# Splitting a two-engine weight conversion into two steps emitted apart, and moving all squares to one engine

## The chip, the cores and the metric

The kernel runs on one core of a Trainium2 chip. Of its engines three matter here: TensorE does the matrix products, ScalarE and VectorE work on whole arrays (tiles). They and the DMA queues, which load and store, run side by side. PSUM is the memory that the products are written to, SBUF the on-chip memory that holds the tiles. "Half clock" is short for a granted TensorE clock near 0.50 in a trace; "issue" of a load is the moment it is sent. The metric is the device time of one execution in microseconds (us). Executions of one kernel usually agree within 1 us, some differ by 3. All ratios are to runs of the kernel before on the same chip, in the same rounds, and each is good to about 0.0015 either way.

## The reference, cut to what matters

```python
# attention without softmax: q, k, v are (8, 8, 576, 64)
kv  = einsum('bhsd,bhse->bhde', k, v)
o   = einsum('bhsd,bhde->bhse', q, kv)
x   = (o / sqrt(mean(o * o, -1) + 1e-6) * g_norm)   # then (4608, 512)
# star-ReLU block: w_in (512, 2048), w_out (2048, 512), given as float64
h   = x @ w_in
g   = s * maximum(h, 0) ** 2 + b
out = g @ w_out
```

The weights arrive as 64-bit floats and have to be turned into 32-bit ones on the chip, once, in 16 tiles of 1 MB. That conversion is what the change is about.

## The kernel before

Both products use a Strassen-like scheme with seven products in place of eight. TensorE works through nine "units" of 512 tokens; in the first, the weights are converted while they are first used. A unit's first product has four blocks s of 512 hidden columns with seven products each (x1, z2, x6, y7, x5, x3, y4). In the traces, each of these is a group of 8 matmul records (4 calls, two records a call) and takes 1.73 us undisturbed.

The conversion of a tile: ScalarE works in place on the high and the low words of the raw tile, VectorE then shifts and adds them into the weight tile:

```python
def round_w(i, dst):
    raw = w_raw.pop(i)
    ...
    nc.scalar.activation(hi, hi, AF.Prelu, scale=2.0**-112, alpha=-(2.0**32))
    nc.scalar.activation(lo, lo, AF.Copy, scale=2.0**-29)
    db = dst.bitcast(U32)
    nc.vector.tensor_scalar(out=db, in0=pairs[:, :, 1], scalar1=3, scalar2=None, op0=ALU.logical_shift_left)
    nc.vector.tensor_tensor(out=db, in0=db, in1=lo, op=ALU.add)
```

Three raw buffers (`tag="raw", bufs=3`) take the loads; the next load is sent after each conversion. Tiles 0 to 7 are w_in (two for each block), 8 to 15 w_out. The products of a block and what they leave to the other engines:

```python
rp = ctx.enter_context(tc.tile_pool(name="rp", bufs=1))      # one buffer for each tag
...
def keep(name, src, tag):                                    # PSUM -> SBUF, ScalarE
    st[name] = rp.tile([P, 2, TB], FP32, name=name, tag=tag)
    nc.scalar.copy(st[name], src)
def x1(): ... mm1_product(1, u, s, st["x"], True);  keep("r1", st["x"], "ra")
def z2(): ... add(t, ps, st["r1"]);                 relu_sq(t, u == 0)
def x6(): ... mm1_product(6, u, s, st["x"], False); keep("r2", st["x"], "rb")
def x5(): ... mm1_product(5, u, s, st["x"], False); keep("r4", st["x"], "ra")
          ... add(t, st["y"], st["r4"]);            relu_sq(t, False)
def x3(): ... # relu on ScalarE, product t*t on VectorE
def y4(): ... add(t, st["y"], st["r2"]);            relu_sq(t, u == 0)
```

x6, x5 and x3 add to the PSUM bank that the copy before them reads, so TensorE can't go on until `r1`, `r2`, `r4` have been copied. `relu_sq(t, True)` is a relu and a square on ScalarE, `relu_sq(t, False)` one fused operation on VectorE. In the traces each of these engines works in the order of emission.

## Time and profile before

| | before |
|---|---|
| median, lowest to highest of 3 runs | 1031.41 us, 1031.16 to 1031.42 |
| span of the profiled execution | 1029.7 us |
| first unit's first product, start to end (35.04 to 113.52 us) | 78.5 us |
| its work at 1.73 us for each of 28 groups | 48.4 us |
| TensorE busy, ScalarE busy, VectorE busy (whole span) | 985.9, 214.4, 444.9 us |

The first row is the time to improve. The third against the fourth is what can be had: about 30 us, all in one early stretch. After it TensorE is busy almost without a break (910.9 of 915.3 us). The bias product (the star-ReLU's b times the output weights) starts where the stretch ends, so its start is the mark by which I compare the traces. The lines of the profile itself are in the prediction.

### The profile page before, as it was taken

What the parts mean: (1) busy time and instruction counts of PE and PEld (TensorE: products, weight loads), DVE (VectorE), ACT (ScalarE), POOL (GpSimd) and SP (SyncE); (2) the same over time, 40 slices, a digit from 0 to 9 for tenths busy, and PEclk for the clock granted to TensorE, in tenths of its full rate; (3) what the DMA queues carried; (4) which work ended last, traced back from release to release, by engine and by line L of the source; (5) the groups of instructions that cost most, each with busy time, mean ns of one, the idle gap of its engine ahead of it and who ended that gap; (6) DMA issues with size and microseconds to landing.
All of it is one profiled execution on the core that took longest, in us unless ns stands there. A gap on an engine that the chain in (4) does not pass through costs nothing.

```text
span 1029.7 us, 13548 instructions
## 1 busy us (share of the span) xinstructions
PE 985.9 (96%) x5824; PEld 860.0 (84%) x5824; DVE 444.9 (43%) x725; ACT 214.4 (21%) x370; POOL 1.6 (0%) x8
## 2 busy tenths in 40 slices
PE   4668899999999999999999999999999999999998
PEld 4557488888888888888888888888888888888887
DVE  0665663445234533453345334433344334524441
ACT  2545512121212121212121212111211121111100
POOL 0000000000000000000000000000000000000000
PEclk9889999999999999999999999999999999999999
DMA  9344781772255125513452325232503250324032
GB/s 249 129 164 141 203 280 52 207 172 82 82 164 134 58 107 153 136 50 123 129 128 65 140 79 147 73 126 76 167 1 123 68 178 1 123 62 143 1 123 82
DMA packets 75244, 121.47 MB, mean 118 GB/s; under 512 B 41904, under 2 KB 49072, under 8 KB 68016
## 3 DMA queue, kind: packets, MB, share of 16 engines
q1 hardware_dynamic: 72048, 118.90, 38.6%
q10 hardware_dynamic: 3136, 1.71, 0.8%
q8 instruction: 46, 0.75, 0.3%
q14 instruction: 14, 0.11, 0.0%
HBM read 103.81 MB, written 16.78 MB: 117 GB/s over the span
## 4 chain that ended last, share of the span: by engine, by line
PE 91%; ACT 3%; DVE 2%; DMA 2%; issue 0%; DVEq 0%
PE x_ps L84 51%; PE y_ps L84 26%; PE z_ps L84 8%; PE qT_ps L295 2%; PE kv_ps L272 2%; PE xT_ps L334 1%; PE b_ps L84 1%; ACT w_raw L163 1%; ACT w_raw L162 1%; DMA kv_sb<-in_v_dram 1%; DMA q_sb<-in_q_dram 1%; DVE wb L168 0%; DMA w_raw<-in_moe_w_in_dram 0%; ACT a L378 0%; ACT a L377 0%
## 5 line engine op out<-in xcount | busy, mean ns | idle before, releaser
L84 PE MATMUL x_ps<-w_sb,a 128*128 128x256 f32 x768 | 172.3, 379 | 0.0
L84 PE MATMUL x_ps<-xs,ws 128*128 128x256 f32 x576 | 142.6, 392 | 18.7 <-ACT r L396 14.8
L84 PEld LDWEIGHTS x_ps<-w_sb,a 128*128 128x128 f32 x768 | 144.3, 190 | 18.9 <-issue 0.2
L84 PE MATMUL y_ps<-w_sb,a 128*128 128x256 f32 x640 | 143.4, 379 | 0.0
L84 PEld LDWEIGHTS x_ps<-xs,ws 128*128 128x128 f32 x576 | 112.6, 196 | 36.6 <-ACT r L396 16.5
L84 PE MATMUL y_ps<-xs,wb 128*128 128x256 f32 x576 | 136.8, 380 | 0.0
L396 ACT COPY r<-x_ps 128x512 f32<-128x512 f32 x108 | 63.2, 585 | 331.4 <-PE x_ps L84 329.5
L84 PEld LDWEIGHTS y_ps<-w_sb,a 128*128 128x128 f32 x640 | 119.4, 190 | 15.2 <-issue 0.2
L84 PEld LDWEIGHTS y_ps<-xs,wb 128*128 128x128 f32 x576 | 110.1, 191 | 15.2
L171 DVE TENSOR_TENSOR a<-y_ps,r 128x512 f32<-128x512 f32 x72 | 49.4, 687 | 132.8 <-ACT r L396 132.8
L84 PE MATMUL x_ps<-xT,wa 128*128 128x256 f32 x288 | 70.6, 390 | 2.1 <-DVE wa L168 2.1
L380 DVE SCALAR_TENSOR_TENSOR a<-a 128x512 f32<-128x512 f32 x100 | 69.2, 692 | 3.4
L84 PE MATMUL x_ps<-xT,ws 128*128 128x256 f32 x288 | 68.8, 382 | 0.7 <-ACT r L396 0.7
L84 PE MATMUL z_ps<-xT,wa 128*128 128x256 f32 x288 | 68.0, 379 | 0.0
L84 PEld LDWEIGHTS x_ps<-xT,wa 128*128 128x128 f32 x288 | 56.7, 197 | 10.7 <-DVE wa L168 2.4
L468 DVE SCALAR_TENSOR_TENSOR or<-x_ps,s_col,b_row 128x256 f32<-128x256 f32 x54 | 26.0, 482 | 89.1 <-PE x_ps L84 89.1
L84 PEld LDWEIGHTS x_ps<-xT,ws 128*128 128x128 f32 x288 | 54.1, 190 | 8.9 <-ACT r L396 1.4
L321 DVE TENSOR_REDUCE ss<-xn 128x8 f32<-128x512 f32 x36 | 24.6, 684 | 85.4 <-ACT xn L319 85.3
L84 PEld LDWEIGHTS z_ps<-xT,wa 128*128 128x128 f32 x288 | 54.7, 190 | 7.4
L429 DVE TENSOR_TENSOR a<-a 128x512 f32<-128x512 f32 x36 | 24.9, 692 | 79.3 <-ACT a L428 79.3
L84 PE MATMUL x_ps<-w_sb,s 128*128 128x256 f32 x256 | 57.8, 380 | 0.0
L84 PEld LDWEIGHTS x_ps<-w_sb,s 128*128 128x128 f32 x256 | 47.6, 190 | 6.1 <-issue 0.2
(80 smaller groups left out, 785.4 us busy)
## 6 DMA issues: line engine op xcount, KB each, us to landing
w_sb<-w SPq DMA_DIRECT2D x56, 1024.0 KB, 4.9
kv_sb<-in_k_dram SPq DMA_DIRECT2D x32, 288.0 KB, 5.2
out_dram<-o SPq DMA_DIRECT2D x72, 128.0 KB, 2.3
q_sb<-in_q_dram SPq DMA_DIRECT2D x68, 128.0 KB, 6.0
w_raw<-in_moe_w_in_dram SPq DMA_DIRECT2D x8, 1024.0 KB, 5.6
w_raw<-in_moe_w_out_dram SPq DMA_DIRECT2D x8, 1024.0 KB, 5.0
kv_sb<-in_v_dram SPq DMA_DIRECT2D x28, 288.0 KB, 6.4
w<-w_up SPq DMA_DIRECT2D x4, 1024.0 KB, 7.8
```

The costliest lines, as they stand in the source:

```text
L84: nc.tensor.matmul(o, lhsT=lhsT, rhs=rhs, start=start, stop=stop, skip_group_check=True)
L162: nc.scalar.activation(hi, hi, AF.Prelu, scale=2.0**-112, alpha=-(2.0**32))
L163: nc.scalar.activation(lo, lo, AF.Copy, scale=2.0**-29)
L171: nc.vector.tensor_tensor(out=o, in0=a, in1=b, op=ALU.add)
L272: nc.tensor.matmul(ps[r][l * HB : l * HB + HB, i, :], lhsT=kv[rows, 0, l, j, :], rhs=kv[rows, 1, l, j, :], start=(j == 0), stop=(j == R - 1),)
L295: nc.tensor.transpose(ps[:, p, :], q_in[c][:, 2 * p : 2 * p + 2, :], ident)
L321: nc.vector.reduce_sum(ss, st["xn"], axis=mybir.AxisListType.X)
L334: nc.tensor.transpose(ps[:, p, :], st["xn"][:, 2 * p : 2 * p + 2, :], ident)
L380: nc.vector.scalar_tensor_tensor(t, t, 0.0, t, ALU.max, ALU.mult)
L396: nc.scalar.copy(st[name], src)
L429: nc.vector.tensor_mul(t, t, t)
L468: nc.vector.scalar_tensor_tensor(o, ps, s_col, other, ALU.mult, ALU.add)
```

## The change

Its intent: ScalarE's half of the conversion ("split") is emitted one tile ahead of VectorE's half ("join"), so that VectorE never waits for it, and the squares leave ScalarE, so that it never waits for VectorE. The core of the diff:

```diff
-    def round_w(i, dst):
+    def split_w(i):
         raw = w_raw.pop(i)
...
         nc.scalar.activation(hi, hi, AF.Prelu, scale=2.0**-112, alpha=-(2.0**32))
         nc.scalar.activation(lo, lo, AF.Copy, scale=2.0**-29)
+        w_bits[i] = pairs
+
+    def join_w(i, dst):
+        bits = w_bits.pop(i)
...
-            out=db, in0=pairs[:, :, 1], scalar1=3, scalar2=None, op0=ALU.logical_shift_left
+            out=db, in0=bits[:, :, 1], scalar1=3, scalar2=None, op0=ALU.logical_shift_left
         )
-        nc.vector.tensor_tensor(out=db, in0=db, in1=lo, op=ALU.add)
+        nc.vector.tensor_tensor(out=db, in0=db, in1=bits[:, :, 0], op=ALU.add)
...
-    def relu_sq(t, on_act):
-        if on_act:
-            nc.scalar.activation(t, t, AF.Relu)
-            nc.scalar.activation(t, t, AF.Square)
-        else:
-            nc.vector.scalar_tensor_tensor(t, t, 0.0, t, ALU.max, ALU.mult)
+    def relu_sq(t):
+        nc.vector.scalar_tensor_tensor(t, t, 0.0, t, ALU.max, ALU.mult)
...
     turn[3]()
+    split(0)
     turn_x[0]()
     product[2]()
     turn_x[1]()
+    join(0)
     product[3]()
+    split(1)
     turn_x[2]()
-    convert(0)
-    turn_x[3]()
     first = {s: mm1(0, s) for s in range(NS)}
     first[0]["x1"]()
+    turn_x[3]()
     x_sums(0)
-    convert(1)
+    join(1)
...
-    at_slot = {0: 2, 2: 3, 4: 4, 7: 5, 9: 6, 12: 7, 15: 8, 18: 9, 20: 10, 22: 11, 24: 12, 26: 13, 27: 14}
+    at_slot = {
+        0: [(split, 2)], 1: [(join, 2), (split, 3)], 3: [(join, 3), (split, 4)], 5: [(join, 4)],
+        6: [(split, 5)], 8: [(join, 5), (split, 6)], 10: [(join, 6)], 11: [(split, 7)],
+        12: [(join, 7)], 13: [(split, 8)], 15: [(join, 8), (split, 9)],
...
+        25: [(join, 13), (split, 14)], 27: [(join, 14), (split, 15)],
+    }
```

A load is still sent after each join, and the raw buffers are still three. The diff also moves some joins to other places between the products (join 5 to slot 8 from 7, join 10 to 19 from 20) and the last turn of x behind the first product.

More of the change, by code (lines that the diff above doesn't have):

```diff
@@ L144, in load_w @@
         w_raw[i] = dst
-    def round_w(i, dst):
+    w_bits = {}
+    def split_w(i):
         raw = w_raw.pop(i)
         if not wide:
-            nc.vector.tensor_copy(out=dst, in_=raw)
+            w_bits[i] = raw
             return
@@ L163, in round_w @@
         nc.scalar.activation(lo, lo, AF.Copy, scale=2.0**-29)
+        w_bits[i] = pairs
+    def join_w(i, dst):
+        bits = w_bits.pop(i)
+        if not wide:
+            nc.vector.tensor_copy(out=dst, in_=bits)
+            return
         db = dst.bitcast(U32)
         nc.vector.tensor_scalar(
-            out=db, in0=pairs[:, :, 1], scalar1=3, scalar2=None, op0=ALU.logical_shift_left
+            out=db, in0=bits[:, :, 1], scalar1=3, scalar2=None, op0=ALU.logical_shift_left
         )
-        nc.vector.tensor_tensor(out=db, in0=db, in1=lo, op=ALU.add)
+        nc.vector.tensor_tensor(out=db, in0=db, in1=bits[:, :, 0], op=ALU.add)
     def add(o, a, b):
@@ L177, with join_w_in @@
     wa, wb, ws = {}, {}, {}
-    def round_w_in(s, lower):
+    def join_w_in(s, lower):
         store, base = (wb, FC // 2) if lower else (wa, 0)
         store[s] = wp.tile([P, KC, 2, P], FP32, name=f"w{'ab'[lower]}_{s}")
-        round_w(base + 2 * s, store[s].rearrange("p c b n -> p (c b n)"))
+        join_w(base + 2 * s, store[s].rearrange("p c b n -> p (c b n)"))
     def sum_w_in(s):
@@ L214, with join_w_out @@
     }
-    def round_w_out(s, lower):
+    def join_w_out(s, lower):
         dst = (w_dn if lower else w_up)[:, 2 * s : 2 * s + 2]
-        round_w(FC + (FC // 2 if lower else 0) + 2 * s, dst.rearrange("p b n -> p (b n)"))
+        join_w(FC + (FC // 2 if lower else 0) + 2 * s, dst.rearrange("p b n -> p (b n)"))
     def sum_w_out(i, fn, a, b):
@@ L407, in z2 @@
             add(t, ps, st["r1"])
-            relu_sq(t, u == 0)
+            relu_sq(t)
         def x6():
@@ L422, in x5 @@
             add(t, st["y"], st["r4"])
-            relu_sq(t, False)
+            relu_sq(t)
         def x3():
@@ L437, in y4 @@
             add(t, st["y"], st["r2"])
-            relu_sq(t, u == 0)
+            relu_sq(t)
         return dict(x1=x1, z2=z2, x6=x6, y7=y7, x5=x5, x3=x3, y4=y4)
@@ L593, in send_w, with split, join @@
             sent[0] += 1
-    def convert(n):
-        s, lower = divmod(n % FC, 2)
+    def split(n):
+        split_w(blocks[n])
+    def join(n):
+        s, lower = divmod(n, 2)
         if n < FC // 2:
-            round_w_in(s, lower)
+            join_w_in(s, lower)
             send_w()
@@ L603, in convert @@
         else:
-            round_w_out(s - NS, lower)
+            join_w_out(s - NS, lower)
             send_w()
@@ L664, in loads @@
             load_q(4 * u + 6)
-    at_slot = {0: 2, 2: 3, 4: 4, 7: 5, 9: 6, 12: 7, 15: 8, 18: 9, 20: 10, 22: 11, 24: 12, 26: 13, 27: 14}
+    at_slot = {
+        0: [(split, 2)], 1: [(join, 2), (split, 3)], 3: [(join, 3), (split, 4)], 5: [(join, 4)],
+        6: [(split, 5)], 8: [(join, 5), (split, 6)], 10: [(join, 6)], 11: [(split, 7)],
+        12: [(join, 7)], 13: [(split, 8)], 15: [(join, 8), (split, 9)],
+        17: [(join, 9), (split, 10)], 19: [(join, 10), (split, 11)],
+        21: [(join, 11), (split, 12)], 23: [(join, 12), (split, 13)],
+        25: [(join, 13), (split, 14)], 27: [(join, 14), (split, 15)],
+    }
     for u in range(U):
@@ L689 @@
             if u == 0 and n in at_slot:
-                convert(at_slot[n])
+                for fn, i in at_slot[n]:
+                    fn(i)
             elif u in kv_due and n == 12:
@@ L696 @@
         if u == 0:
-            convert(15)
+            join(FC - 1)
             for i in range(2):
```

## The prediction

> **What bounds the kernel now.** I read the page first. TensorE is busy 96% of the span, but the slices show where the other 4% lies:
>
> ```profile
> PE 985.9 (96%) x5824; PEld 860.0 (84%) x5824; DVE 444.9 (43%) x725; ACT 214.4 (21%) x370; POOL 1.6 (0%) x8
> PE   4668899999999999999999999999999999999998
> PEclk9889999999999999999999999999999999999999
> ```
>
> Only the first slices (26 us each) are thin. The stretch view confirms it; its columns are stretch, length, busy time of each engine, granted clock, DMA share, GB/s:
>
> ```profile
> 66.00:68.00 2.00, 0.00 (x0) 0.00 (x0) 1.74 (x3) 0.23 (x1) 0.00 (x0) 0.50 0.87 319
> 113.69:1029.00 915.31, 910.88 (x5392) 797.45 (x5391) 388.31 (x645) 159.12 (x292) 0.00 (x0) 1.00 0.37 111
> ```
>
> From 113.69 us to the end TensorE is busy 910.9 of 915.3 us at full clock, so nothing is to be had there, and what ends sooner before it should come off the total one for one. Before it lies the first unit's first product, 35.04 to 113.69 us: 78.65 us for 28 groups of 8 matmuls, each 1.73 us where nothing disturbs it (starts at 54.70, 56.42, 58.15): 48.4 us of work, some 30 us lost. The waits of the first 145 us (total, times, longest) say to whom:
>
> ```profile
> ACT a L377 <- DVE a L171: 20.2, 6, 4.7
> PE x_ps L84 <- ACT r L396: 15.5, 4, 7.8
> DVE wb L165 <- ACT w_raw L162: 10.2, 4, 2.9
> PE x_ps L84 <- DVE ws L174: 3.8, 1, 3.8
> ```
>
> TensorE waits for a copy of ScalarE, ScalarE for VectorE, VectorE for ScalarE. The timeline shows one turn of that wheel:
>
> ```profile
> 59.91 0.63 ACT L377 ACTIVATE a<-a 128x512 f32<-128x512 f32 x1 [2.76 <-DVE a L171]
> 61.11 1.09 ACT L162 ACTIVATE w_raw<-w_raw 128x1024 f32<-128x1024 f32 x1
> 62.11 1.12 ACT L163 ACTIVATE w_raw<-w_raw 128x1024 uint32<-128x1024 uint32 x1
> 62.24 0.69 DVE L165 TENSOR_SCALAR wb<-w_raw 128x1024 uint32<-128x1024 uint32 x1 [2.36 <-ACT w_raw L162]
> 63.26 1.22 DVE L168 CUSTOM_DVE_ANT_0 wb<-w_raw,wb 128x2048 uint16<-128x2048 uint16 x1 [0.33 <-ACT w_raw L163]
> 67.06 0.68 DVE L171 TENSOR_TENSOR a<-y_ps,r 128x512 f32<-128x512 f32 x1
> 67.77 0.63 ACT L377 ACTIVATE a<-a 128x512 f32<-128x512 f32 x1 [4.55 <-DVE a L171]
> 68.97 0.57 ACT L396 COPY r<-x_ps 128x512 f32<-128x512 f32 x1
> 69.59 3.78 PE L84 MATMUL x_ps<-xs,ws 128*128 128x256 f32 x8 [7.83 <-ACT r L396]
> ```
>
> TensorE had finished by 61.8 us what the copy at 68.97 reads. But the copy stood in ScalarE's queue behind a square that needed VectorE's addition, and that addition stood in VectorE's queue behind a conversion that needed ScalarE's two operations. Four such waits of 15.5 us, 3.8 us for the first sums, and five restarts at half clock. The last from the starts of the groups: 35.04 to 38.26, 43.94 to 49.41 (two groups), 69.59 to 76.01 (two), 89.04 to 92.55, 105.81 to 109.29, each less 1.73 a group: 1.5 + 2.0 + 3.0 + 1.8 + 1.75 = 10 us. 15.5 + 3.8 + 10 = 29.3 of the 30 us.
>
> **What the Trainium skill says.** (1) "TensorE: Matmul & The Clock Gate", the specifications and Part 1: ScalarE and VectorE run strictly first in, first out, so the order of emission decides who waits. The trace agrees: the copy at 68.97 us came 7 us after its data. (2) The same Part 1: after an idle window of about 3.4 us the matmul clock is halved, and returns after one busy window. The trace agrees: granted clock 0.50 at 66 to 68 us, then 3.78 us for 8 matmuls. (3) "ScalarE: Activation LUTs", What ACT_TABLE_LOAD costs: an activation with immediates takes 186 ns + 0.833 ns an element, so 1.04 us for 1024; the trace has 1.14 and 1.15 us on these interleaved words, starting 1.02 us apart. I use the trace. (4) "VectorE: DVE Perf Modes", Mode 2×_2P: a one-source fp32 operation from SBUF to SBUF can deliver two elements a cycle, one with two tensor sources can't. The shift of 1024 words takes 0.69 us, as long as an addition of 512: they agree.
>
> **The change part by part.**
> Removed: on ScalarE 8 times relu and square, 8 x (0.66 + 0.54) = 9.6 us by their starts. Added: on VectorE 8 times the fused square that is already there (0.69 us, 0.61 to the next start): 4.9 us. The wait of ScalarE for VectorE (20.2 us) goes altogether: every operation left on ScalarE in this stretch waits for TensorE or for a load.
> Moved: the two ScalarE operations of a tile ("split", 2.05 us) go one tile ahead of VectorE's two ("join": 0.82 + 1.14 = 1.96 us, from the starts 44.91, 45.73, 46.88). The kernel still has three raw buffers, and the next load is still issued when a join ends (35.01 is the end of the first), landing 4.8 to 5.3 us later (5.8 for one). The first three land at 21.8, 24.7 and 27.4 us.
>
> New loads of the engines in the stretch. VectorE: 15 joins 29.4, 4 weight sums of 2.55 each 10.2, 4 input sums 2.6, and for each of four groups three add-and-square pairs of 1.33 and a product of 0.61: 18.4. Together 60.6 us. ScalarE: 14 splits 28.7, 12 copies and 4 relus at 0.5 to 0.6: 37 us. TensorE 48.4. VectorE thus becomes nearly the bound, but its last two joins may lie under the bias product, so some 57 us count.
>
> I walk the queues in their new order with those spacings (each line: what, from where, when).
> Start. Split 0 goes ahead of the first xT copy: 26.77, so that copy moves from 26.77 to 28.81 and the third chunk's norm ends at 32.05 instead of 30.0. Join 0 follows it: 31.97 to 34.02. First product at 34.05 (was 35.04), at half clock to 37.4. Then the last transpose, its copy 38.05 to 38.7, the input sums 38.75 to 41.4, and only behind them join 1, 41.3 to 43.35. The first two weight sums end at 44.8, so the third group of 8 starts at 44.9, where it was 43.94: 1 us worse. Half clock again; second block's x1 at 52.2.
> Second block. VectorE: sums 45.9, pair 47.2, joins 2 and 3 to 51.25, sums to 53.8, pair, join 4 to 57.2; TensorE finds all its operands and runs through: x6 at 59.1 (ws was there at 52.7), x5 62.55, next x1 64.3.
> Third block. Join 5 ends at 62.7, sums at 65.2, join 6 at 67.3, join 7 at 70.6. Its x1 64.3, x6 71.2 with sums of 64.1, no wait. Split 9 waits for load 9 (67.3 + 5.1 = 72.4), ends 74.5, and holds the copy to 75.0: x5 at 75.05, 0.4 us lost.
> Fourth block. x1 76.75, x3 78.5, z2, y4, x6 to 85.4, y7 to 87.1. Join 8 ends at 78.5, join 9 at 80.45, join 10 at 83.75. Split 11 waits for its load until 83.5, so relu ends at 86.15 and split 12 at 88.2; the copy ends at 88.7: x5 at 88.75, 1.65 us lost. Split 13 (load at 88.75) ends at 90.85, copy 91.35: x3 at 91.4, 0.9 us lost. y4 to 94.9.
> Join 14 ends at 101.75 and join 15 at 103.7. The bias product starts at 94.9 and asks for these two after 10.3 and 12.0 us (1.72 us for 4 matmuls): 105.2 and 106.9. No wait.
>
> Sum: the bias product starts at 94.9 instead of 113.7, 18.8 us sooner. 1031.4 - 18.8 = 1012.6, say 1012.5 us.
>
> **The rivals.**
> (a) TensorE never idles after 44.9 us. For it: the lost 2.95 us hang on loads landing within 1 to 2 us. Then 26 groups, 44.9 us, and 1.7 us of half clock: 91.5, 22 us saved, 1009 us. Against it: three buffers with a tile split ahead leave at most one load between a join's end and the next use.
> (b) VectorE becomes the bound, or ScalarE blocks: a split waiting for its load at the queue's head holds the copies that TensorE needs. The fixed 5 us from issue to landing speak for it. If each of splits 8 to 14 held its copy by 1 us more, saved are 12 to 14 us: 1018 us.
> (c) The gain is given back in the second product: the stores of the weights, and the sum that waits 2.34 us for them (at 137.19), hang on the last join but one, which now ends 6.9 us after the bias product starts (before 7.5). 16 us from there to that sum as before, and 5 more until its product can run: 122.6, against 127 asked. So no wait; if it came, it would cost 2 to 4 us: 1016 us.
> (d) The start loses more than 1 us because the norm stands behind split 0: 1014 us.
>
> **Range and chances.** The centre is 1012.5. (a) sets the floor near 1009, (b), (c) and (d) the other side: 1009 to 1017.5 should hold it 8 times in 10. Over 2% needs 20.6 us, that is less than 1.2 us of the 2.95 lost, or an earlier third group: 0.2. Within 2%: 0.79. Slower by 2%: 0.01, for nothing new reaches the 915 us after the stretch.
>
> **What would show it right or wrong.** Right: the wait of ScalarE's square for VectorE is gone; the 7.8, 4.2 and 2.7 us waits of TensorE for the copy shrink to below 2 us each; the first wait for the weight sums is still there and longer, near 5 us; only two stretches at half clock are left (34 to 38, 45 to 48); VectorE is busy some 85% between 45 and 83 us; the bias product starts near 95 us. Wrong: VectorE's joins wait for splits (rival b), waits of 3 us and more that halve the clock a third time, or a bias product that waits for the last joins; or a start of the bias product near 95 but a total that does not follow (rival c).

## The result, and the profile after

| | before | after |
|---|---|---|
| median of the rounds' runs | 1031.31 us | 1016.93 us (1016.48 to 1017.16) |
| span of the profiled execution | 1029.7 us | 1014.7 us |
| first product, start to end | 35.04 to 113.52 us | 33.39 to 98.51 us |
| from there to the end of the span | 916.2 us | 916.2 us |

The ratio is 0.986, 95% interval 0.9843 to 0.9877. A ratio here is the mean time of one kernel's fast runs over that of the other's of the same rounds, so it isn't quite the ratio of the medians. The gain is 14.4 us by the medians, inside the predicted range, but 4.4 us short of the 18.8 us of its sum. In the two profiled executions (1031.52 and 1016.48 us) the bias product starts 15.0 us sooner. The last row of the table says where all of it lies: nothing changed after the stretch.

The page of the changed kernel:

```profile
PE 982.4 (97%) x5824; PEld 858.3 (85%) x5824; DVE 449.8 (44%) x733; ACT 205.6 (20%) x354; POOL 1.6 (0%) x8
PE   4698999999999999999999999999999999999998
PEclk9799999999999999999999999999999999999999
```

VectorE got 4.9 us more and ScalarE 8.8 us less, and the thin slices are now three in place of five. The stretch after the mark, as before (stretch, length, busy times, clock):

```profile
98.51:1014.00 915.49, 911.04 (x5393) 797.61 (x5391) 387.88 (x645) 154.94 (x288) 0.00 (x0) 1.00 0.37 111
```

The waits of the first 145 us (total, times, longest):

```profile
PE x_ps L84 <- DVE ws L184: 5.2, 1, 5.2
ACT r L402 <- DVE a L181: 4.9, 3, 2.5
PE x_ps L84 <- ACT r L402: 3.6, 3, 2.1
```

The row of 20.2 us in which ScalarE's squares waited for VectorE's additions is gone, and TensorE's wait for the copies fell from 15.5 to 3.6 us. The second line is new to me: the copies themselves now wait for VectorE's additions. No copy reads what an addition writes. It is the other way round: the addition of the block before reads the buffer that the copy is about to overwrite. The timeline of the third block shows it, ScalarE first, then VectorE and TensorE:

```profile
73.27 1.18 ACT L164 ACTIVATE w_raw<-w_raw 128x1024 f32<-128x1024 f32 x1 [1.19 <-DMA w_raw<-in_moe_w_out_dram]
74.35 1.14 ACT L165 ACTIVATE w_raw<-w_raw 128x1024 uint32<-128x1024 uint32 x1
76.76 0.59 ACT L402 COPY r<-x_ps 128x512 f32<-128x512 f32 x1 [1.27 <-DVE a L181]
```

```profile
75.99 0.68 DVE L181 TENSOR_TENSOR a<-y_ps,r 128x512 f32<-128x512 f32 x1
```

```profile
77.40 3.41 PE L84 MATMUL x_ps<-xs,ws 128*128 128x256 f32 x8 [2.13 <-ACT r L402]
80.60 2.21 PE L84 MATMUL x_ps<-xT,wa 128*128 128x256 f32 x8
```

The copy r2 of the third block could have run at 75.5 us, behind split 9. It ran at 76.76, when the second block's last addition, which reads r2 in the same single buffer, was through VectorE's queue. TensorE waited 2.13 us and then ran at half clock. The chain of waits of the changed kernel (start, length, what) tells what VectorE was doing so late:

```profile
77.32 0.70 DVE w_up L175
...
78.14 1.24 DVE w_up L178
79.40 4.92 DMA w_raw<-in_moe_w_out_dram
84.33 1.14 ACT w_raw L164
85.48 1.03 ACT w_raw L165
86.50 0.49 ACT a L434
87.02 0.69 DVE a L435
87.71 0.61 DVE a L181
88.34 0.69 DVE a L386
89.04 0.61 DVE w_dn L175
89.67 1.22 DVE w_dn L178
90.90 0.61 DVE a L181
...
91.59 0.59 ACT r L402
92.17 1.06 ACT w_raw L164
93.24 1.06 ACT w_raw L165
94.31 0.59 ACT r L402
...
94.95 1.99 PE x_ps L84 x8
```

Read it from the bottom. x3 of the fourth block waits for copy r4, that for split 13 ahead of it in ScalarE's queue, that for copy r2, which waits for an addition (90.90) to free its buffer. The addition stands behind join 11, a square, and a product that needed ScalarE's relu (86.50), which stood behind split 11, which waited for its load, which was sent only when join 8 ended (79.40). Ahead of that, from 62.35 us on, the chain stays on VectorE. TensorE does not appear in it between 62.35 and 94.95 us: in the last two blocks of this trace TensorE's own time hardly counts.

So my theory A: what the prediction missed is the single buffer of each kept copy, which ties ScalarE's copies to VectorE's long queue. Rival B: VectorE's queue is the bound in itself, and the buffers only show it. Rival C: the loads, with three raw buffers and some 5 us from sending to landing, set the pace. Besides these I wanted to know which half of the change gave the gain.

### The profile page after: what moved, and what is told of

Same layout as the page of the kernel before. It is cut to its first block, busy times and chain, and to the rows that moved or that the text cites. A ratio compares the mean times of both kernels' runs of the same rounds, so it can differ in the third digit from the quotient of the medians.

```text
span 1014.7 us, 13541 instructions
## 1 busy us (share of the span) xinstructions
PE 982.4 (97%) x5824; PEld 858.3 (85%) x5824; DVE 449.8 (44%) x733; ACT 205.6 (20%) x354; POOL 1.6 (0%) x8
## 4 chain that ended last, share of the span: by engine, by line
PE 93%; DVE 3%; DMA 2%; ACT 1%; issue 0%; DVEq 0%; ACTq 0%
PE x_ps L84 51%; PE y_ps L84 27%; PE z_ps L84 9%; PE qT_ps L305 2%; PE kv_ps L282 2%; PE xT_ps L344 1%; PE b_ps L84 1%; DMA kv_sb<-in_v_dram 1%; DMA q_sb<-in_q_dram 1%; DMA w_raw<-in_moe_w_out_dram 0%; DMA kv_sb<-in_k_dram 0%; PE x_ps L320 0%; DVE wb L178 0%; DVE ws L184 0%; ACT w_raw L164 0%
## 5 line engine op out<-in xcount | busy, mean ns | idle before, releaser
L84 PE MATMUL x_ps<-xs,ws 128*128 128x256 f32 x576 | 139.6, 386 | 8.1 <-DVE ws L184 5.2
L386 DVE SCALAR_TENSOR_TENSOR a<-a 128x512 f32<-128x512 f32 x108 | 74.7, 692 | 3.7
```

Of the source, the lines that this page charges most:

```text
L84: nc.tensor.matmul(o, lhsT=lhsT, rhs=rhs, start=start, stop=stop, skip_group_check=True)
L386: nc.vector.scalar_tensor_tensor(t, t, 0.0, t, ALU.max, ALU.mult)
```

## The experiments

Twelve runs, each compared with runs of the kernel before on the same chip. All results were correct.

**Own buffers for r2 and r4.** In the first unit they use the two output-row buffers, which are idle there.

```diff
+            if u == 0 and name != "r1":
+                st[name] = outp.tile([P, 2, TB], FP32, name=name, tag="o2" if name == "r2" else "o1")
+            else:
                 st[name] = rp.tile([P, 2, TB], FP32, name=name, tag=tag)
```

> The changed kernel, but in the first unit the kept copies r4 and r2 get two buffers each of their own (of the output rows, idle there), so a copy no longer waits for VectorE's addition to read the block before's. Theory A (the single buffer, behind VectorE's long queue, made the wait of 2.13 us and the third restart at half clock of 1.8 us): the wait at the third block's x5 falls below 1.2 us, the restart at half clock goes, the fourth block's waits fall too, the bias product starts about 2.4 us sooner: 1014.5 us, ratio to before 0.9837. Rival B (VectorE's queue itself is the pace, the buffer only shows it): the wait comes back elsewhere in the fourth block and less than 0.8 us is won: 1016.2 us or more. Rival C (splits waiting for their loads hold the copies): the copy now waits behind split 9 as long as before, nothing is won.

Measured: 1015.04 us, ratio 0.9838 (0.9823 to 0.9853), bias product at 96.69 us. TensorE's timeline in the third and fourth block:

```profile
76.03 1.99 PE L84 MATMUL x_ps<-xs,ws 128*128 128x256 f32 x8 [0.76 <-ACT r L405]
77.86 1.89 PE L84 MATMUL x_ps<-xT,wa 128*128 128x256 f32 x8
...
89.62 1.99 PE L84 MATMUL x_ps<-xs,ws 128*128 128x256 f32 x8 [0.77 <-ACT r L405]
```

The wait fell from 2.13 to 0.76 us and no half clock followed. The two ratios' intervals overlap a little, but the bias product came 1.8 us sooner than in the changed kernel's trace (98.51), and 1.9 us sooner than in a second trace of it further down (98.62). Theory A is right on the buffers; rival C, as the only cause, is out. What is left here (a copy behind split 9, which waited 2.2 us for its load) is rival C's.

**The squares alone.** The kernel before with `relu_sq(t, False)` everywhere, the conversion undivided at its old slots.

> The kernel before with one part of the change alone: all squares on VectorE, conversion undivided at its old slots. If the ring ScalarE to VectorE to ScalarE is what cost, this cuts one of its two links: the copies no longer stand behind squares, but a join still waits for a split emitted just ahead of it. I expect 5 to 9 us of the 14.4: 1024 us, ratio 0.993. If the squares were all of it: 1017 us. If only the split ahead mattered: 1030 us or more.

Measured: 1017.77 us, ratio 0.9865 (0.985 to 0.9879). I expected half of the gain and found nearly all of it.

**The layout alone.** The changed kernel with relu and square of a11 and a12 of the first unit back on ScalarE.

> The changed kernel with the other part undone: relu and square of a11 and a12 of the first unit back on ScalarE, the split still one tile ahead. VectorE has 5 us less, but ScalarE's queue again waits for VectorE's additions, and the copies stand behind them. I expect 5 to 9 us of the 14.4: 1024 us, ratio 0.993; 1017 us if the layout alone were the gain; 1031 us if the gain needs both parts.

Measured: 1018.04 us, ratio 0.987 (0.9854 to 0.9887). Again nearly all of it; neither differs from the whole change (0.986) by more than the interval. The expectation was wrong in both cases, in the same way: I added up two links of one ring, but a ring needs to be cut only once. The waits of these two show what each keeps; first the squares alone, then the layout alone:

```profile
ACT r L396 <- DVE a L171: 12.9, 4, 6.7
PE x_ps L84 <- ACT r L396: 6.0, 3, 4.0
```

```profile
ACT a L387 <- DVE a L181: 11.0, 5, 5.8
PE x_ps L84 <- ACT r L406: 5.5, 4, 2.6
```

With the squares on VectorE the wait comes back as copies that wait for a buffer (12.9 us); with the squares on ScalarE they still wait for additions (11.0 us), but a join no longer waits for the split just ahead of it: the 10.2 us of the kernel before for the tiles wb are down to 0.4 (`DVE wb L175 <- ACT w_raw L164`). TensorE's wait falls from 15.5 to about 6 us by either. The layout here is the split ahead together with the moved places; which of the two gave the gain is not shown.

**Join 1 ahead of the input sums.**

```diff
-    x_sums(0)
     join(1)
+    x_sums(0)
```

> The changed kernel with join 1 emitted ahead of the input sums instead of behind them: VectorE idles 3.1 us there, waiting for the last xT copy, while split 1 is done at 36.2 us. The join should run at 35.3 to 37.4 us, the weight sums end about 1.95 us sooner, x6 of the first block start at 42.4 instead of 44.4 us, load 4 be issued 5 us sooner. As VectorE's queue is nearly full from there on, all of 1.9 us should reach the end: 1015 us, ratio 0.984. If the pace of the later blocks is set by the loads or the r buffers alone, less than 1 us is won.

Measured: 1013.41 us, ratio 0.9822 (0.9807 to 0.9837), 0.0038 less than the change alone. x6 of the first block started at 42.56 us as expected. In the profiled executions the gain is 2.0 us (1014.45 against 1016.48), as expected; by the ratios it is 3.9 us. The profiled run is the slowest of the four (1012.31 to 1014.45), and its trace shows a likely reason: x5 of the fourth block ran 3.48 us at half clock after a wait of 2.49 us, the copy r4 waited for it (1.53 us), and x3 for the copy. That x6 and y7 together took 5.21 us in place of 6.56 at the start needn't be part of the gain: the next experiment takes away more there and wins little.

**Matmuls of no use in the idle gap**, twice. Into a spare PSUM tile, after the first block's z2:

```diff
+            if u == 0 and s == 0:
+                warm = ps_t.tile([P, 2, TB], FP32, name="warm_ps", tag="t")
+                for n in range(20):          # second run: 10
+                    matmul(warm[:, 0], w_in_of(2, s, 0, 0), x_of(2, u, 0), True, True)
```

> The changed kernel with 20 matmuls (128x256) of no use after the first block's z2, into a spare PSUM tile, so that TensorE does not idle the 5 us before the first weight sums are ready. The granted clock should stay at 1.00 and the next two groups of 8 take 3.5 us instead of 6.56 us. If TensorE's own time paces the later blocks, the 3.1 us reach the end: 1013.8 us, ratio 0.983. If VectorE's queue and the single r buffers pace them (theory A), VectorE had only 0.9 us of idle time between 53 and 60 us to give: the wait at the third block grows by 2 us or so and at most 1 us is won: 1016 us, ratio 0.985.

Measured: 1017.96 us, ratio 0.9867 (0.9852 to 0.9882). This run was badly sized: the 20 calls are 40 records and ran until 49 us, past the point where x6 could start. So once more with 10:

> The run with matmuls of no use again, with 10 in place of 20: each is two passes in the trace, so the 20 took 8.8 us and held the first block's x6 back to 49.1 us. Ten take 4.3 us and end before the first weight sums. The next two groups of 8 should take 3.5 us in place of 6.6 us. If TensorE's time paces the later blocks: 3.1 us won, 1013.8 us, ratio 0.983. If VectorE's queue and the r buffers pace them: the wait at the third block grows to 4 us and at most 1 us is won: 1016 us or more, ratio 0.985 or more.

Measured: 1018.03 us, ratio 0.9865 (0.9848 to 0.9881). The trace shows the trade plainly:

```profile
39.64 4.48 PE L84 MATMUL warm_ps<-xT,wa 128*128 128x256 f32 x20
44.97 1.96 PE L84 MATMUL x_ps<-xs,ws 128*128 128x256 f32 x8 [0.85 <-DVE ws L184]
46.77 1.89 PE L84 MATMUL y_ps<-xs,wb 128*128 128x256 f32 x8
...
76.61 1.99 PE L84 MATMUL x_ps<-xs,ws 128*128 128x256 f32 x8 [2.88 <-ACT r L402]
...
91.74 3.68 PE L84 MATMUL x_ps<-xs,ws 128*128 128x256 f32 x8 [2.77 <-ACT r L402]
```

```profile
95.51 0.59 ACT L402 COPY r<-x_ps 128x512 f32<-128x512 f32 x1 [1.72 <-PE x_ps L84]
```

The two groups ran at full clock in 3.5 us, so the second block's x1 came 5.26 us after x6 and not 8.29. TensorE gave these 3 us back, waiting 2.88 us in the third and 2.77 us in the fourth block for copies. TensorE's speed in the first block doesn't set the pace; VectorE and the buffers do. One thing in this trace blurs the result: the last group shown ran at half clock, and there it does count, for the copy r4 (the single line) waited 1.72 us for it and x3 for the copy. Without that the bias product would have started near 98.0 us (an estimate, 99.70 less 1.72), against 98.51 and 98.62 in the two traces of the changed kernel: about half a microsecond won, not 3.1. VectorE is busy for 34.89 of the 38 us from 45 to 83 us in the changed kernel, 36.07 in this one.

**A fourth place for raw tiles.** Tiles 3, 7 and 11 land in the half of the output weights' tile that isn't written yet; everything after tile 3 is sent one join sooner where a place is free.

```diff
+        if wide and sent[0] in (3, 7, 11):
+            dst = w_dn[:, 4:].rearrange("p f n -> p (f n)").bitcast(U32)
+        else:
             dst = convp.tile([P, 4 * R * D], U32, name="w_raw", tag="raw", bufs=3)
...
-    for _ in range(3):
+    for _ in range(4):
         send_w()
```

> The changed kernel with a fourth place for raw tiles (tiles 3, 7 and 11 land in a part of the output weights' tile that is not yet written). Rival C (splits wait for their loads): the four waits of splits for loads, 3.7 us in all, go, the copies r4 of the fourth block come 0.7 to 1 us sooner each: about 1.5 us won, 1015.4 us. Theory A: the wait of 2.13 us at the third block is VectorE's and stays (split 9 ended at 75.5 us, the copy ran at 76.8 us), so less than 2 us is won. Nothing won at all would mean the loads never mattered.

Measured: 1014.52 us, ratio 0.9833 (0.9818 to 0.9847). That is more than expected, and its trace didn't explain it: the waits for the copies were the same as in the changed kernel, and only less time ran at half clock. That could be luck. So I ran the changed kernel and this one again side by side, as control and repeat.

> The changed kernel once more, unaltered, as a control beside the next run. Its first trace had the wait of 2.13 us at the third block and then 1.8 us of half clock. If the restart belongs to the wait, it is there again, and the times lie within 0.5 us of 1016.9 us. If it depends on where the wait falls[...], this trace may lack it, and the times spread by some 2 us.

> The fourth place for raw tiles once more. In its first trace TensorE waited as long for the copies as in the changed kernel (3.7 against 3.6 us), and what it won lay in half clock alone (none after the third block's wait, 1.5 us less after the first sums). If the won 2.4 us are the loads' doing, the ratio stays near 0.9833 and lies below the control's on this chip by 0.002 or more. If they were the luck of the clock gate, the two runs come within 0.001 of each other.

Measured: the control 1017.0 us, ratio 0.9864 (0.9848 to 0.9881); the fourth place 1014.73 us, ratio 0.9832 (0.9819 to 0.9846). The difference of 0.0032 holds, so the loads do count. The two traces, first the control, then the fourth place:

```profile
77.48 1.99 PE L84 MATMUL x_ps<-xs,ws 128*128 128x256 f32 x8 [2.13 <-ACT r L402]
79.32 1.89 PE L84 MATMUL x_ps<-xT,wa 128*128 128x256 f32 x8
...
92.34 1.99 PE L84 MATMUL x_ps<-xs,ws 128*128 128x256 f32 x8 [2.50 <-ACT r L402]
...
98.62 1.88 PE L84 MATMUL b_ps<-w_up,b_sq 128*128 128x512 f32 x4
```

```profile
77.39 3.49 PE L84 MATMUL x_ps<-xs,ws 128*128 128x256 f32 x8 [2.13 <-ACT r L405]
...
91.27 1.98 PE L84 MATMUL x_ps<-xs,ws 128*128 128x256 f32 x8
93.97 1.99 PE L84 MATMUL x_ps<-xT,ws 128*128 128x256 f32 x8 [0.73 <-ACT r L405]
```

In the second trace the fourth block's wait for r2 is gone: split 11 no longer waits for its load, so the chain shown above lost that link. The trace to compare it with is the changed kernel's first, which had the same half clock in the third block: there that copy ran at 91.59 us, here at 90.61, and the bias product starts at 97.53 in place of 98.51. So in this pair 1.0 us is the loads'. And the control taught me more than I asked: the same kernel, the same wait of 2.13 us, but no half clock after it, so TensorE was 1.8 us ahead of the first trace. It then waited 2.50 us in the fourth block where the first trace had 0.78, and the bias product started at 98.62, against 98.51 us. The half clock of the third block costs nothing at the end, because the wait after it takes the difference (in the fourth block no such wait follows, as the run with 10 useless matmuls showed).

**Two and three of the places mended together.**

> Two of the mended places together: own buffers for r2 and r4, and join 1 ahead of the input sums. Alone they gave 0.9838 and 0.9822 where the change gave 0.986. If they are different waits their gains add up: 0.980, 1011 us. If both only shift the same wait on VectorE's queue, no more than the better of them: 0.982.

Measured: 1011.0 us, ratio 0.9799 (0.9785 to 0.9814). The changed kernel's first run gave 0.986; own buffers took 0.0022 off and join 1 0.0038, together 0.9800. The gains add up within the 0.0015 of each ratio: rival B in its plain form (one queue, one wait, only shifted) is out.

> The changed kernel with all three: own buffers for r2 and r4, join 1 ahead of the input sums, a fourth place for raw tiles. The first two together gave 0.9799; in their trace splits wait 11.3 us for loads and TensorE 3.3 us for copies behind them. If the loads are what is left (rival C, now uncovered), most of these 3.3 us go: 1008.5 us, ratio 0.9775. If VectorE's queue is what is left, less than 1 us is won: 0.979.

Measured: 1008.9 us, ratio 0.9778 (0.9762 to 0.9795), faster than both kernels and faster than before by more than 2%. In the waits of its first product the copies cost TensorE little:

```profile
PE x_ps L84 <- DVE xs L187: 2.1, 1, 2.1
PE x_ps L84 <- ACT r L408: 1.3, 1, 1.3
PE y_ps L84 <- DVE a L184: 0.6, 1, 0.6
```

With two mended places the copies had still cost 3.3 us. The bias product starts at 89.38 us here; its first product takes 56.2 us, with 48.4 us of work.

**The own buffers in the kernel before.**

> The kernel before with only the own buffers for r2 and r4 in the first unit. There the copies stand behind squares that wait for the same VectorE additions anyway, so the buffers should be worth little as long as the ring is uncut: under 2 us, ratio 0.998 or more. If the single buffers had been the bottleneck of the kernel before too, the ratio would come near 0.99 or below.

Measured: 1031.47 us, ratio 0.9999 (0.9982 to 1.0015): nothing. TensorE's wait for the copies is still 14.8 us there. The single buffers became a bound only once the ring was cut.

## Why the prediction was right or wrong, point by point

- **Where the time was.** Right: from the bias product to the end both kernels take 916.2 us, and the whole gain lies ahead of it. Rival (c), that the second product would give it back, did not happen: the sum behind the stores started at 119.75 us, straight after VectorE's operation before it, and what x6 of the second product needs was ready at 124.65 us (122.6 predicted), 6 us before TensorE asked for it at 130.8.
- **The ring of ScalarE and VectorE.** Right as a mechanism: the 20.2 us of waiting squares are gone. What I had not said is that either half of the change cuts it: 0.9865 and 0.987 alone, 0.986 together. One reading in the prediction was short: the copy at 68.97 us came 9 us after its data, not 7, for the group that it reads was followed by the next at 59.88; 61.8 is the end of that next group.
- **The start.** Right within 0.7 us: the first product at 33.39 (34.05 predicted; the first norm began 0.5 us earlier in this run), x6 at 44.37 (44.9). The 5.2 us wait for the first sums came as said, and join 1 ahead of the input sums, which shortens it, had the lowest ratio of the single edits (0.9822; the next is 0.9832, within its interval).
- **The second block.** Right: no wait until its end; x1 at 52.66 (52.2).
- **The third block: the step that failed.** "Split 9 ... holds the copy to 75.0: x5 at 75.05, 0.4 us lost". TensorE lost 2.13 us. My walk let a copy go as soon as ScalarE and TensorE were ready, and checked its buffer nowhere. With one buffer for r2, the copy may not start before the addition of the block before has read it, and the walk's own spacings put that addition at 75.1 us (join 7 at 70.6, then sums of 2.55, a product of 0.61 and a pair of 1.33).
- **The fourth block: the same term.** "The copy ends at 88.7: x5 at 88.75" while the same spacings put the addition that reads that buffer at 90.05 us (relu at 86.15, then 0.61, 1.33 and a join of 1.96). Working the walk on from there, copy r2 runs at 90.8 to 91.35, split 13 to 93.4, copy r4 to 93.9, x3 to 95.7 and y4 to 97.4 us in place of 94.9. So the missing buffer is worth 2.5 us of the sum. Own buffers, which take it away, measured a ratio lower by 0.0022, which is 2.3 us; in the traces the bias product came 1.8 us sooner. The remaining 1.1 us to the 98.51 of the trace is mostly VectorE's queue, by reading and not by experiment: the addition came at 90.82 and not 90.05, and from there each step ran slightly longer. The largest single piece of it that I can name is a stop of 0.56 us inside join 5; the profile puts it down to a ScalarE copy that the join doesn't read, and I did not find the cause.
- **Half clock.** Wrong in count: I had said that only two such stretches would remain, and the first trace has a third. But the control shows that this one doesn't matter at the end. The wait before it, 2.13 us, was also just above the 2 us that I had named as the sign of being right.
- **The bound.** "VectorE thus becomes nearly the bound" was right in kind: 34.89 of 38 us busy, 92% where I said 85%, and full clock for TensorE in the first block bought about half a microsecond. But it acts through the buffers of the copies and through the loads, and both can be lifted without taking work from VectorE. Rival (b) named the right place, copies that hold TensorE, with a cause, splits waiting for loads, that is only part of it.
- **The sum and the range.** The mark of the kernel before, 113.69, comes from the view of the chain, which puts it 0.17 us later than the timeline (113.52) in which the walk counts; against 113.52 the walk saves 18.6 us, and the trace 15.0. The measured 1016.93 lies only 0.6 us inside the upper end of the range. That end was set by rivals (b) to (d), none of which names the buffer, so that the range held is partly luck.

What stays open: how much the fourth place for raw tiles wins through the loads and how much through the clock. Its two traces differ in this, while the times agree; the one like-for-like pair gives 1.0 us to the loads, out of 3.3 us by the ratios.

## What to carry to other kernels

When two engines wait for each other in turn, cut the ring once and look again: here the second cut was worth little, and the next bound was a buffer with a single copy that was harmless while the ring held everything back. When you walk a schedule by hand, write down for each write not only when its inputs are there, but when the last reader of its buffer is done. An engine that gets faster in one place without the end moving has shown you that it isn't the pace there.

## What the Trainium skill lacked or had wrong

- "TensorE: Matmul & The Clock Gate", Part 1 and the table under "Why this matters for your kernels", puts the loss of full clock at an idle window of about 3.4 us and advises against gaps over about 3 us. A wait of 2.13 us was followed by a group of 8 that took 3.2 to 3.3 us at half clock in two traces, by two groups of 2.6 us in a third, and by none in a fourth; in one trace a wait of 2.88 us left the clock alone and one of 2.77 us halved it. The kernel before had it already: 2.73 us of waiting, then a group of 3.48 us. So shorter gaps than the page warns of can cost, though not every time; what decides is not shown here.
- "ScalarE: Activation LUTs", What ACT_TABLE_LOAD costs, gives 186 ns + 0.833 ns an element, so 1.04 us for 1024 elements. On every second 32-bit word, in place, the traces have 1.08 to 1.24 us, and the next operation mostly starts 0.98 to 1.08 us after the one before; with the overlap of 93 ns that the section gives it would be 0.95 (an estimate from its figures). The section does not speak of spaced elements.
- No page that I read says how a ring of waits between two in-order queues is told from a single long wait. "Perfetto Trace Analysis", Identifying Dependency Chains, says to look up what a wait waits for; here that gave a copy (15.5 us), but the gain came from two engines further back (20.2 and 10.2 us).
